# First pair in a list of its own ahead of the loop, second pair's turns placed earlier in PE's list, and the small tables made on GpSimd

## The chip, the cores and the metric

The kernel runs on one core of one Trainium2 chip. The metric is the device time of one execution in microseconds (us). Before the change it is 121.83 us, the median of 8 runs (121.37 to 122.72).

Engines are called by short names here: PE (TensorE, matrix multiplies), DVE (VectorE), ACT (ScalarE), POOL (GpSimd) and SP (SyncE, which issues DMAs here and nothing else). Each works through its own list of instructions in order, and waits where an instruction needs what another engine or a DMA has not delivered.

## What is computed

A linear attention with decay (RWKV5) feeds a soft mixture of experts. Cut to what matters:

```python
# r, k, v: (4, 8, 768, 48) float32;  w, u: (8, 48)
for t in range(S):
    cur = einsum('bhd,bhe->bhde', u * k[:, :, t], v[:, :, t])
    y[:, :, t] = einsum('bhd,bhde->bhe', r[:, :, t], state + cur)
    state = w[..., None] * state + einsum('bhd,bhe->bhde', k[:, :, t], v[:, :, t])

x = y.transpose(0, 2, 1, 3).reshape(3072, 384)
logits = x @ phi                                  # 3072 x 32 slots
d = softmax(logits, axis=0)                       # dispatch
slot_in = (d.T @ x).reshape(8, 4, 384)
slot_out[e] = relu(slot_in[e] @ w1[e]) @ w2[e]    # w1: 8 x 384 x 1024, w2: 8 x 1024 x 384
out = softmax(logits, axis=1) @ slot_out          # 3072 x 384
```

Each softmax adds 1e-9 to its sum. The inputs are k, r, v (14.2 MB), w1 and w2 (25.2 MB) and some small ones; the output is 4.7 MB.

## The kernel before

The recurrence is not run step by step. For two heads at a time (a *pair*, 96 channels) k and r are scaled by powers of the decay, so that the state's decay becomes a product of two tables, and chunks of 128 positions are handled by matrix multiplies. A batch has four pairs (q = 0 to 3), four batches make 16 pairs, m = 0 to 15. A pair has 768 positions in two *halves* of three chunks; the halves are numbered i = 0 to 31.

The steps of a pair or half, by the names of their helpers:

- `tt(j, q)` and `ex(j, q)` make the decay tables, once for each q and for k (j = 0) and r (j = 1): a product on DVE (L193) and an exponential on ACT (L197), into `W`. They need `lnw`, the logarithm of w spread over all partitions by `spread` (L182 on PE, L183 on ACT).
- `scale(m, j)` (L233) multiplies k or r by its table into `kr`, on DVE for the first pair and on POOL for all others.
- `t_pe`, `t_evac`: the *turns*. PE transposes `kr` into T0 or T1 (L240), and ACT copies it into `kT` or `rT` (L246). `b_pe`, `b_evac` turn kT back (L252 on PE, L257 on DVE) into `kn`. `prod_f` (L262, DVE) multiplies the turned k and r.
- `v_cast` casts v to bf16 (L273 on POOL for the first pair, L275 on ACT for the others); `v_pe`, `v_evac` bring it into order (L289 on PE, L295 on ACT) as `vn`.
- `a_pe`, `mask_f`: products of kT and rT within a chunk (L304, PE), masked on DVE (L309) into `AT`.
- `m_pe`, `z_evac`: states (L319, L330) and the u term (L334) in `Mb`; DVE multiplies them by the table `zt` (L346) and makes the diagonal part `dv` (L347). `zt[:, q, 2]` is the table's decayed part: ACT copies `zt[:, q, 0]` scaled by `wT` (L552). `wT` and `ucol` come from w and u through one small transpose (L208) and a few tiny operations (`wu_steps`, L206).
- `y_pe`, `y_evac`: the output of a half (L357, L368, L370, then ACT L377).

The kernel writes the order of every engine's list out by hand: `O(...)` keeps instructions in the order in which the program records them. The main loop (L499) runs from i = -5 to 31. In turn i it handles a_pe and m_pe of half i + 1, y_pe of half i, v_pe of half i + 2, scale and turns of the pairs two or three ahead, and from the second batch on a piece of routing (`route`: logits, exponentials, dispatch sums) for the batch before. The negative turns are the ramp: each helper is called only if its index exists. Three small tables say what else a turn records: `T_AT` the decay tables, `Z_AT` the decayed parts of zt, and `W_AT` how many expert weights POOL issues.

Loads: SP issues all of k, r and v. A batch lies in one of three `raw` buffers; the fourth batch goes into the first one's buffer and is issued at turn 3. The sixteen expert weights (768 KB each in bf16; the DMA casts from f32) are issued by POOL, w1 into `w_all` (L140), w2 into the second and third raw buffer (L143). Ahead of the first, at turn 12, POOL copies one element of the last batch's k into `guard` (L576), so that it waits for that load. The last weight is cut into three pieces, issued behind the loop (L581).

Behind the loop come the two expert products (L628, L665), where PE takes the experts in the order of their loads, the scaling of the slots (L676), and the output in eight pieces (L689 to L709).

`keep_warm(n)` (L146) issues n matmuls of zeros whose result is not used.

Of the kernel before, what the change touches and what calls it, by code (L numbers as in the profile page):

```python
# [9 lines left out]
def kernel(  # L10
# [41 lines left out]
    def O(ins):  # L52
        return tc.keep_in_program_order(ins)
# [57 lines left out]
    O(dve.memset(warm, 0.0))  # L111
    O(dve.memset(one_f, 1.0))
    zt = cst.tile([128, nQ, 3, P2], f32, name="zt")
    O(dve.memset(zt[:], 0.0))

    def load_kr(which, src, b, h0, h1):
        O(sp.dma_start(out=raw_of(which, b).rearrange("p (h x) -> p h x", h=H)[:, h0:h1, :],
# [28 lines left out]
    def keep_warm(n, bank=Yb, data=None):  # L146
        data = warm if data is None else data
        for _ in range(n):
            O(pe.matmul(bank[:, 0:512], data[:, 0:128], data[:, 0:512], start=True, stop=True))
# [25 lines left out]
        O(dve.memset(t[:].rearrange("p a j (e s) -> p (a j e) s", s=64)[:, :, D:64], 0.0))  # L175
    ident = cst.tile([128, 128], bf, name="ident")
    O(dve.tensor_copy(ident[:], ident_f))

    keep_warm(4)

    def spread(bank, a, z):
        O(pe.matmul(bank[:, 0:z - a], one_f, w_row[:, a:z], start=True, stop=True))  # L182
        O(act.activation(out=lnw[:, a:z], in_=bank[:, 0:z - a], func=AF.Ln))  # L183
# [7 lines left out]
    def tt(j, q):  # L191
        e = (sk, sr)[j]
        O(dve.tensor_mul(W[j][:, q], lnw[:, None, q * P2:(q + 1) * P2].to_broadcast([128, J, P2]),  # L193
                         e[:, :, None].to_broadcast([128, J, P2])))

    def ex(j, q):
        O(act.activation(out=W[j][:, q], in_=W[j][:, q], func=AF.Exp))  # L197

    tt(0, 0)
    tt(1, 0)  # L200
    spread(Vb, P2, H * D)
    ex(0, 0)
    ex(1, 0)
    wT = cst.tile([128, nQ], f32, name="wT")

    def wu_steps(n):  # L206
        if n == 0:
            O(pe.transpose(Mb[:, 0:8], wu[:], ident_f[0:8, 0:8]))  # L208
            O(act.activation(out=wT[:], in_=Mb[:, 0:4], func=AF.Ln))
            O(act.activation(out=wT[:], in_=wT[:], func=AF.Exp, scale=float(T)))  # L210
            O(dve.tensor_copy(wuT[:], Mb[:, 0:8]))
        if n == 1:
            O(dve.tensor_mul(ucol[0:64, :, 0], wuT[0:64, 0:4], wuT[0:64, 4:8]))
            O(dve.tensor_mul(ucol[64:128, :, 1], wuT[64:128, 0:4], wuT[64:128, 4:8]))

    O(pool.memset(zt[0:64, :, :, 0:D], 1.0))
    O(pool.memset(zt[64:128, :, :, D:P2], 1.0))
    ones = cst.tile([128, 128], bf, name="ones")
    Le_t = [cst.tile([128, L, 128], bf, name=f"Le{j}") for j in range(2)]
    phi_s = cst.tile([128, nM, ES], bf, name="phi_s")  # L220
# [7 lines left out]
    def scale(m, j):  # L228
        b, q = divmod(m, nQ)
        kr = kr_t[m % NKR]  # L230
        src = raw_of(j, b).rearrange("p (h j d) -> p j h d", h=H, j=J)[:, :, 2 * q:2 * q + 2, :]
        eng = dve if m == 0 else pool
        O(eng.tensor_mul(kr[:, j].rearrange("p j (h s) -> p j h s", s=64)[:, :, :, 0:D], src,  # L233
                          W[j][:, q].rearrange("p j (h d) -> p j h d", h=2)))

    def t_pe(m, j):
        kr = kr_t[m % NKR]
        bank = (T0, T1)[j]
        for x in range(J):
            O(pe.transpose(bank[:, x * C:(x + 1) * C], kr[:, j, x, :], ident[:]))  # L240
# [8 lines left out]
    def b_pe(m):  # L249
        kT = st["kT", m]  # L250
        for c in range(nC):
            O(pe.transpose(T0[:, c * C:(c + 1) * C], kT[:, c * C:(c + 1) * C], ident[:]))  # L252

    def b_evac(m):
        kn = wk.tile([128, nC, C], bf, name="kn", bufs=2)
        st["kn", m] = kn
        O(dve.tensor_copy(kn[:].rearrange("p c t -> p (c t)"), T0[:, 0:S]))  # L257
# [34 lines left out]
    def v_evac(i):  # L292
        vn = wk.tile([128, L, 2, D], bf, name="vn", bufs=3)
        st["v", i] = vn
        O(act.copy(vn[:].rearrange("p c e d -> p (c e d)"), Vb[:, 0:L * P2]))  # L295
# [146 lines left out]
    def route(i, part):  # L442
# [23 lines left out]
        if s < 2 * L:  # L466
            xt_ev(*ch[s])

    pend = []
    W_AT = {12: 1, 13: 1, 14: 1, 15: 1, 17: 1, 19: 1, 20: 1, 22: 1, 23: 1, 25: 1, 26: 5}  # L470
    T_AT = {-4: [(tt, 0, 1), (tt, 1, 1), (ex, 0, 1), (tt, 0, 2)], -3: [(ex, 1, 1), (ex, 0, 2)],
            -1: [(tt, 1, 2), (ex, 1, 2)], 0: [(tt, 0, 3), (ex, 0, 3)], 1: [(tt, 1, 3), (ex, 1, 3)]}
    Z_AT = {-3: 0, -1: 1, 1: 2, 2: 3}
    nw = 0
    n0, n1 = nG - 2, nG - 1
    Wf = [t[:].rearrange("p q j d -> p (q j d)") for t in W]
# [18 lines left out]
                O(pe.matmul(lg[:, c, :], xs[:, n - n0, mi, c, :], phi_s[:, mi, :],  # L495
                            start=(mi == 0 and c == 0), stop=(mi == nM - 1), skip_group_check=True))

    keep_warm(5)
    for i in range(-5, nH):  # L499
        mu, odd = divmod(i, 2)  # L500
        if 0 <= i + 1 < nH:
            a_pe(i + 1)
            mask_f(i + 1)
        if pend:
            disp_ev(*pend.pop())
        if i == nH - 1:
# [1 line left out]
            disp(n0 - 1, ds_t)  # L508
            le_t(n0 - 1)
            let_ev(n0 - 1, None, dve)  # L510
        if 0 <= i < nH:
            y_pe(i)
            y_evac(i)
        if 0 <= i + 2 < nH:
            v_pe(i + 2)
            v_evac(i + 2)
        if 0 <= i + 1 < nH:
            m_pe(i + 1)
            z_evac(i + 1)
        if odd == 0 and 0 <= mu + 1 < nU:  # L520
# [9 lines left out]
        if 0 <= mu + 2 < nU:  # L530
            t_pe(mu + 2, odd)
            route(i, 1)
            t_evac(mu + 2, odd)
            if odd and i < 0:
                b_pe(mu + 2)
                b_evac(mu + 2)
        else:
            route(i, 1)
        if odd == 0 and 0 <= mu + 2 < nU:
# [5 lines left out]
            turn(n1, (0, 1), T1, act)  # L545
        for f, j, q in T_AT.get(i, ()):
            f(j, q)
        if i in (-4, -3):
            wu_steps(i + 4)
        if i in Z_AT:  # L550
            q = Z_AT[i]
            O(act.activation(out=zt[:, q, 2, :], in_=zt[:, q, 0, :], func=AF.Copy, scale=wT[:, q:q + 1]))  # L552
        if i == 2:
            O(pool.memset(ones[:], 1.0))
            for t in Le_t:
# [184 lines left out]
```

The softmax here doesn't subtract the row's maximum and nothing guards it: scores larger than these inputs give would overflow.

## Time and profile before

| what | value |
|---|---|
| median of 8 runs | 121.83 us |
| the profiled execution's own time | 121.37 us |
| its span in the trace | 119.6 us |
| busy in the span: PE, DVE, ACT, POOL | 101.4, 94.9, 83.6, 59.2 us |
| DMA written: by SP's queue (q1), by POOL's (q0) | 16.03 MB, 15.34 MB |
| read from HBM, written to HBM | 39.38 MB, 4.72 MB |
| first half's output (L357) starts | 14.15 us |
| first weight load issued by POOL | 37.99 us |
| first expert product (L628) starts | 91.22 us |
| last matmul of the second expert product | 103.02 us |

The span begins with the first instruction and ends with the last; 1.77 us of the execution's own time lie around it. Busy times of different engines overlap, so they say how full an engine is and not what sets the end. What sets the end is read from three views: the *chain of waits*, which starts at the last instruction and follows back, step by step, what released it; the *windows*, which give each engine's busy time, the granted PE clock, the busy share of the 16 DMA engines and the GB/s that they wrote in a stretch of the span; and the *timeline*, which lists instructions in order with the idle time ahead of each and what ended it. Where an instruction waited for several things, the idle time is put down to one of them.

### The profile page before, as it was taken

The numbers are of one execution on the slowest core, as the hardware profiler recorded it, in microseconds if no ns is written. First come the engines' busy times: TensorE is split into PE (matmuls) and PEld (weight loads), VectorE is DVE, ScalarE is ACT, GpSimd is POOL, SyncE is SP. The second block draws the span as 40 slices with busy tenths as digits, with TensorE's granted clock in tenths as the row PEclk, the third lists the DMA queues.
The fourth block names the chain that finished last, engine by engine and source line by source line (L and its number), as shares of the span: only waits on it lengthen the run. The fifth ranks groups of instructions, "written<-read, shape, count | busy, mean of one in ns | idle before, by whom it ended". The sixth has DMA issues, their size and how long they took to land.

```text
span 119.6 us, 4336 instructions
## 1 busy us (share of the span) xinstructions
PE 101.4 (85%) x1797; PEld 81.7 (68%) x1797; DVE 94.9 (79%) x187; ACT 83.6 (70%) x183; POOL 59.2 (50%) x70
## 2 busy tenths in 40 slices
PE   5897877799999999999999999999979996795000
PEld 1455766578988888898888888888865686682000
DVE  6889999999999999899999899999943510499000
ACT  4259887998979988888898988988954500398000
POOL 7426744699999999796877592111000000011100
PEclk9999999999999999999999999999999999999755
DMA  3999999999999999999999999999999998179991
GB/s 98 341 345 367 377 374 371 348 389 362 319 387 381 343 218 223 211 219 210 221 212 219 214 214 216 216 213 214 215 216 213 220 205 146 18 288 386 428 407 70
DMA packets 20797, 31.79 MB, mean 266 GB/s; under 512 B 1129, under 2 KB 17898, under 8 KB 20650
## 3 DMA queue, kind: packets, MB, share of 16 engines
q0 software_dynamic: 2960, 15.34, 57.1%
q1 hardware_dynamic: 17648, 16.03, 39.7%
q8 instruction: 14, 0.23, 0.7%
q10 hardware_dynamic: 170, 0.15, 0.4%
q14 instruction: 5, 0.04, 0.1%
HBM read 39.38 MB, written 4.72 MB: 369 GB/s over the span
## 4 chain that ended last, share of the span: by engine, by line
PE 39%; DMA 21%; DVE 19%; ACT 7%; issue 6%; DVEq 0%; POOLq 0%; ACTq 0%
DMA raw<-in_moe_w_dram 21%; PE Vb L289 6%; PE T L240 5%; PE Ab L304 4%; PE Yb L357 4%; DVE W L193 3%; DVE prod L262 3%; PE Mb L330 3%; PE T L252 3%; DVE AT L309 2%; DVE raw L691 2%; PE Yb L370 2%; ACT rT L246 2%; DVE dv L347 2%; PE Xb L392 2%
## 5 line engine op out<-in xcount | busy, mean ns | idle before, releaser
L233 POOL TENSOR_TENSOR kr<-raw,W 128x576 bf16<-128x576 f32 x30 | 41.9, 1413 | 13.7 <-ACT W L197 5.0
L309 DVE TENSOR_TENSOR AT<-Ab,mask_ut 128x768 bf16<-128x768 f32 x32 | 30.3, 947 | 0.8 <-PE Ab L304 0.6
L289 PE MATMUL Vb<-v_bf,Q 128*128 128x96 bf16 x288 | 17.5, 206 | 0.4 <-ACT vn L295 0.4
L240 PE MATMUL T<-ident,kr 128*128 128x128 bf16 x192 | 16.6, 225 | 0.9 <-POOL kr L233 0.9
L289 PEld LDWEIGHTS <-Q 128*128 128x128 bf16 x288 | 15.8, 98 | 1.8 <-issue 0.4
L246 ACT COPY kT<-T 128x768 bf16<-128x768 bf16 x16 | 12.8, 801 | 4.5 <-PE T L240 3.3
L246 ACT COPY rT<-T 128x768 bf16<-128x768 bf16 x16 | 12.8, 803 | 3.4 <-PE T L240 2.8
L262 DVE TENSOR_TENSOR prod<-T,kT 128x768 bf16<-128x768 bf16 x16 | 15.2, 949 | 0.0
L347 DVE TENSOR_TENSOR dv<-vn,Mb 128x288 bf16<-128x288 bf16 x32 | 14.1, 442 | 0.0
L295 ACT CAST vn<-Vb 128x288 bf16<-128x288 f32 x32 | 13.4, 419 | 0.1
L240 PEld LDWEIGHTS <-kr 128*128 128x128 bf16 x192 | 12.2, 100 | 1.7 <-POOL kr L233 1.0
L346 DVE TENSOR_TENSOR Z<-Mb,zt 128x288 bf16<-128x288 f32 (+1 forms) x32 | 12.7, 398 | 0.8
L377 ACT CAST x<-Yb 128x288 bf16<-128x288 f32 x32 | 13.1, 409 | 0.2 <-PE Yb L370 0.2
L709 POOL DMA_DIRECT2D out_dram<-W x1 | 0.6, 552 | 24.9 <-DVE W L691 24.9
L304 PE MATMUL Ab<-rT,kT 64*128 64x128 bf16 x192 | 10.9, 219 | 2.0 <-DVE AT L309 2.0
L330 PE MATMUL Mb<-vn,kn 128*128 128x96 bf16 (+2 forms) x80 | 11.2, 238 | 0.0
L357 PE MATMUL Yb<-vn,AT 128*128 128x48 bf16 x192 | 10.3, 185 | 0.1
L275 ACT CAST v_bf<-raw 128x576 bf16<-128x576 f32 x15 | 10.2, 678 | 0.0
L143 POOL DMA_DIRECT2D raw<-in_moe_w_dram x10 | 5.5, 558 | 7.8 <-DMA raw<-in_moe_w_dram 2.9
L357 PEld LDWEIGHTS <-AT 128*128 128x128 bf16 x192 | 7.1, 96 | 3.3
L304 PEld LDWEIGHTS <-kT 64*128 64x128 bf16 x192 | 5.5, 94 | 5.5 <-DVE AT L309 1.9
L370 PE MATMUL Yb<-dv,ident 128*128 128x288 bf16 x32 | 9.1, 284 | 0.2
(143 smaller groups left out, 220.3 us busy)
## 6 DMA issues: line engine op xcount, KB each, us to landing
w_all<-in_moe_w_dram POOLq DMA_DIRECT2D x8, 768.0 KB, 13.7
raw<-in_moe_w_dram POOLq DMA_DIRECT2D x7, 768.0 KB, 18.8
raw<-in_v_dram SPq DMA_DIRECT2D x12, 288.0 KB, 7.3
raw<-in_r_dram SPq DMA_DIRECT2D x8, 288.0 KB, 5.0
raw<-in_k_dram SPq DMA_DIRECT2D x2, 1152.0 KB, 9.9
raw<-in_r_dram SPq DMA_DIRECT2D x2, 1152.0 KB, 9.4
raw<-in_k_dram SPq DMA_DIRECT2D x7, 288.0 KB, 5.7
out_dram<-raw POOLq DMA_DIRECT2D x1, 1536.0 KB, 6.7
```

The source lines that it names most:

```text
L233: O(eng.tensor_mul(kr[:, j].rearrange("p j (h s) -> p j h s", s=64)[:, :, :, 0:D], src, W[j][:, q].rearrange("p j (h d) -> p j h d", h=2)))
L240: O(pe.transpose(bank[:, x * C:(x + 1) * C], kr[:, j, x, :], ident[:]))
L246: O(act.copy(t[:].rearrange("p (s j) -> p s j", j=J), bank[:, 0:S].rearrange("p (j s) -> p s j", j=J)))
L262: O(dve.tensor_mul(pr[:].rearrange("p (s j) -> p s j", j=J), T1[:, 0:S].rearrange("p (j s) -> p s j", j=J), st["kT", m][:].rearrange("p (s ...
L289: O(pe.matmul(Vb[:, c * P2:(c + 1) * P2], Q3[:, o:o + C], vb[:, :, g, j, :], start=(j == 0), stop=(j == JV - 1)))
L295: O(act.copy(vn[:].rearrange("p c e d -> p (c e d)"), Vb[:, 0:L * P2]))
L304: O(pe.matmul(Ab[:, e, c * C:(c + 1) * C], kT[s, t], rT[s, t]))
L309: O(dve.tensor_mul(AT[:], Ab[:, :, 0:T].rearrange("p e (c t) -> p e c t", c=L), mask_ut[:, None, None, :].to_broadcast([128, 2, L, C])))
L330: O(pe.matmul(o, kn[:, g * L + c, :], vc, start=first, stop=True, skip_group_check=True))
L347: O(dve.tensor_mul(dv[:], st["v", i][:].rearrange("p c e d -> p (c e) d"), Mb[:, 288:288 + 2 * L, None].to_broadcast([128, L * 2, D])))
L357: O(pe.matmul(Yb[:, o:o + D], AT[:, e, c, :], vn[:, c, e, :], start=first, stop=False, skip_group_check=True))
L377: O(act.copy(st["x", n][:, :, q * P2:(q + 1) * P2], Yb[:, 0:L * P2].rearrange("p (c e) -> p c e", c=L)))
```

## The change

The ramp is taken out of the loop. The loop now starts at i = 0, and what the negative turns did (with some of turn 0) is written out ahead of it as one list. In that list:

- `prod_f(0)` stands ahead of `b_evac(0)` and the first `mask_f` directly behind them; a_pe and mask_f of half 1, y_pe of half 0, m_pe of half 1 and the turns and `b_pe` of pair 1 have places of their own. `t_pe(1, 0)` is recorded ahead of `a_pe(1)`, `t_pe(1, 1)` behind `y_pe(0)`.
- The tables of q = 2 (`tt(0, 2)`, `tt(1, 2)`) are recorded behind the second mask_f and the second z_evac.
- The small transpose stands between the turns of k and r. Its result is copied once to `wuT` by DVE; `wT` is made from wuT, and the two products into `ucol` are POOL's, no longer DVE's.
- The decayed part of zt for q = 0 is made in the list, and for q = 1, 2, 3 at the ends of turns 0, 1, 2 (before at turns -3, -1, 1, 2).

Ahead of the list, DVE no longer clears all of zt early; it clears the two thirds that need it behind the copy of the identity, and POOL's two memsets of ones cover the same two thirds and stand behind the first v_cast. `ex(0, 0)` is recorded ahead of the second `spread`. The zero matmuls are two and three, before four and five. In `W_AT` the issues from turn 17 on stand one turn later. DMAs on SP's and ACT's queues are as before, in the same order.

```diff
--- before.py
+++ after.py
@@ -111,7 +111,6 @@
     O(dve.memset(warm, 0.0))
     O(dve.memset(one_f, 1.0))
     zt = cst.tile([128, nQ, 3, P2], f32, name="zt")
-    O(dve.memset(zt[:], 0.0))
 
     def load_kr(which, src, b, h0, h1):
         O(sp.dma_start(out=raw_of(which, b).rearrange("p (h x) -> p h x", h=H)[:, h0:h1, :],
@@ -175,8 +174,9 @@
         O(dve.memset(t[:].rearrange("p a j (e s) -> p (a j e) s", s=64)[:, :, D:64], 0.0))
     ident = cst.tile([128, 128], bf, name="ident")
     O(dve.tensor_copy(ident[:], ident_f))
-
-    keep_warm(4)
+    O(dve.memset(zt[:, :, 0:2, :], 0.0))
+
+    keep_warm(2)
 
     def spread(bank, a, z):
         O(pe.matmul(bank[:, 0:z - a], one_f, w_row[:, a:z], start=True, stop=True))
@@ -198,23 +198,15 @@
 
     tt(0, 0)
     tt(1, 0)
+    ex(0, 0)
     spread(Vb, P2, H * D)
-    ex(0, 0)
     ex(1, 0)
+    keep_warm(3)
     wT = cst.tile([128, nQ], f32, name="wT")
 
-    def wu_steps(n):
-        if n == 0:
-            O(pe.transpose(Mb[:, 0:8], wu[:], ident_f[0:8, 0:8]))
-            O(act.activation(out=wT[:], in_=Mb[:, 0:4], func=AF.Ln))
-            O(act.activation(out=wT[:], in_=wT[:], func=AF.Exp, scale=float(T)))
-            O(dve.tensor_copy(wuT[:], Mb[:, 0:8]))
-        if n == 1:
-            O(dve.tensor_mul(ucol[0:64, :, 0], wuT[0:64, 0:4], wuT[0:64, 4:8]))
-            O(dve.tensor_mul(ucol[64:128, :, 1], wuT[64:128, 0:4], wuT[64:128, 4:8]))
-
-    O(pool.memset(zt[0:64, :, :, 0:D], 1.0))
-    O(pool.memset(zt[64:128, :, :, D:P2], 1.0))
+    def decay(q):
+        O(act.activation(out=zt[:, q, 2, :], in_=zt[:, q, 0, :], func=AF.Copy, scale=wT[:, q:q + 1]))
+
     ones = cst.tile([128, 128], bf, name="ones")
     Le_t = [cst.tile([128, L, 128], bf, name=f"Le{j}") for j in range(2)]
     phi_s = cst.tile([128, nM, ES], bf, name="phi_s")
@@ -467,10 +459,9 @@
             xt_ev(*ch[s])
 
     pend = []
-    W_AT = {12: 1, 13: 1, 14: 1, 15: 1, 17: 1, 19: 1, 20: 1, 22: 1, 23: 1, 25: 1, 26: 5}
-    T_AT = {-4: [(tt, 0, 1), (tt, 1, 1), (ex, 0, 1), (tt, 0, 2)], -3: [(ex, 1, 1), (ex, 0, 2)],
-            -1: [(tt, 1, 2), (ex, 1, 2)], 0: [(tt, 0, 3), (ex, 0, 3)], 1: [(tt, 1, 3), (ex, 1, 3)]}
-    Z_AT = {-3: 0, -1: 1, 1: 2, 2: 3}
+    W_AT = {12: 1, 13: 1, 14: 1, 15: 1, 18: 1, 20: 1, 21: 1, 23: 1, 24: 1, 26: 1, 27: 5}
+    T_AT = {0: [(tt, 0, 3), (ex, 0, 3)], 1: [(tt, 1, 3), (ex, 1, 3)]}
+    Z_AT = {0: 1, 1: 2, 2: 3}
     nw = 0
     n0, n1 = nG - 2, nG - 1
     Wf = [t[:].rearrange("p q j d -> p (q j d)") for t in W]
@@ -495,10 +486,62 @@
                 O(pe.matmul(lg[:, c, :], xs[:, n - n0, mi, c, :], phi_s[:, mi, :],
                             start=(mi == 0 and c == 0), stop=(mi == nM - 1), skip_group_check=True))
 
-    keep_warm(5)
-    for i in range(-5, nH):
+
+    scale(0, 0)
+    scale(0, 1)
+    v_cast(0)
+    O(pool.memset(zt[0:64, :, 0:2, 0:D], 1.0))
+    O(pool.memset(zt[64:128, :, 0:2, D:P2], 1.0))
+    tt(0, 1)
+    tt(1, 1)
+    t_pe(0, 0)
+    t_evac(0, 0)
+    O(pe.transpose(Mb[:, 0:8], wu[:], ident_f[0:8, 0:8]))
+    t_pe(0, 1)
+    t_evac(0, 1)
+    O(dve.tensor_copy(wuT[:], Mb[:, 0:8]))
+    ex(0, 1)
+    b_pe(0)
+    a_pe(0)
+    v_pe(0)
+    prod_f(0)
+    b_evac(0)
+    mask_f(0)
+    O(pool.tensor_mul(ucol[0:64, :, 0], wuT[0:64, 0:4], wuT[0:64, 4:8]))
+    O(pool.tensor_mul(ucol[64:128, :, 1], wuT[64:128, 0:4], wuT[64:128, 4:8]))
+    scale(1, 0)
+    ex(1, 1)
+    scale(1, 1)
+    v_evac(0)
+    O(act.activation(out=wT[:], in_=wuT[:, 0:4], func=AF.Ln))
+    O(act.activation(out=wT[:], in_=wT[:], func=AF.Exp, scale=float(T)))
+    decay(0)
+    m_pe(0)
+    z_evac(0)
+    t_pe(1, 0)
+    t_evac(1, 0)
+    a_pe(1)
+    mask_f(1)
+    v_pe(1)
+    v_evac(1)
+    y_pe(0)
+    y_evac(0)
+    tt(0, 2)
+    t_pe(1, 1)
+    t_evac(1, 1)
+    ex(0, 2)
+    v_cast(1)
+    m_pe(1)
+    z_evac(1)
+    b_pe(1)
+    tt(1, 2)
+    ex(1, 2)
+    b_evac(1)
+    scale(2, 0)
+
+    for i in range(nH):
         mu, odd = divmod(i, 2)
-        if 0 <= i + 1 < nH:
+        if 0 < i < nH - 1:
             a_pe(i + 1)
             mask_f(i + 1)
         if pend:
@@ -508,13 +551,13 @@
             disp(n0 - 1, ds_t)
             le_t(n0 - 1)
             let_ev(n0 - 1, None, dve)
-        if 0 <= i < nH:
+        if i > 0:
             y_pe(i)
             y_evac(i)
         if 0 <= i + 2 < nH:
             v_pe(i + 2)
             v_evac(i + 2)
-        if 0 <= i + 1 < nH:
+        if 0 < i < nH - 1:
             m_pe(i + 1)
             z_evac(i + 1)
         if odd == 0 and 0 <= mu + 1 < nU:
@@ -531,9 +574,6 @@
             t_pe(mu + 2, odd)
             route(i, 1)
             t_evac(mu + 2, odd)
-            if odd and i < 0:
-                b_pe(mu + 2)
-                b_evac(mu + 2)
         else:
             route(i, 1)
         if odd == 0 and 0 <= mu + 2 < nU:
@@ -545,11 +585,8 @@
             turn(n1, (0, 1), T1, act)
         for f, j, q in T_AT.get(i, ()):
             f(j, q)
-        if i in (-4, -3):
-            wu_steps(i + 4)
         if i in Z_AT:
-            q = Z_AT[i]
-            O(act.activation(out=zt[:, q, 2, :], in_=zt[:, q, 0, :], func=AF.Copy, scale=wT[:, q:q + 1]))
+            decay(Z_AT[i])
         if i == 2:
             O(pool.memset(ones[:], 1.0))
             for t in Le_t:
```

## The prediction

> **What bounds the kernel now.** I read the chain of waits first, then the windows, because a share of busy time says nothing about which wait ends last. The chain's pieces from 77 us on:
>
> ```profile
> 77.55 24.86 DMA raw<-in_moe_w_dram
> ...
> 102.44 0.24 PE Xb L665
> ...
> 103.22 0.43 DVE W L676
> ```
>
> Columns are start, length, what. From 77.55 to 102.4 the chain is one weight load; PE's last expert (L665) starts when it lands, and 17.2 us of scaling and output stand behind it. Is that load late because it was issued late, or because the DMA engines are full? The windows answer (stretch and length; busy us of PE, PEld, DVE, ACT, POOL with their instructions; granted clock; DMA share; GB/s written):
>
> ```profile
> 12.00:15.00 3.00, 2.60 (x55) 2.37 (x54) 2.86 (x6) 2.63 (x6) 2.09 (x2) 1.00 1.11 378
> ...
> 24.00:27.00 3.00, 2.91 (x59) 2.29 (x57) 3.00 (x8) 2.80 (x7) 3.00 (x4) 1.00 1.09 389
> ...
> 45.00:48.00 3.00, 2.93 (x58) 2.35 (x54) 2.94 (x6) 2.73 (x6) 3.00 (x3) 1.00 1.02 212
> ...
> 75.00:78.00 3.00, 2.99 (x61) 2.57 (x58) 3.00 (x7) 2.76 (x7) 0.47 (x2) 1.00 1.03 211
> ...
> 96.00:99.00 3.00, 2.63 (x82) 2.26 (x74) 0.14 (x2) 0.00 (x0) 0.00 (x0) 1.00 1.04 208
> 99.00:102.00 3.00, 2.30 (x24) 1.92 (x24) 0.00 (x0) 0.00 (x0) 0.00 (x0) 1.00 0.72 128
> ```
>
> The share is above 1 in every 3 us from 3 to 99 us (between 1.01 and 1.17). Up to some 42 us the engines bring k, r and v, then the weights at a flat 211 to 225 GB/s written, which is twice that read, as the weights are cast from f32 to bf16 on the way. The bytes agree: 14.2 MB of k, r, v and 12.6 MB of weights written by 102 us. It is one gapless stream, and its sum sets 102.4. Third, the timelines of PE and of POOL near it (start, length, what, and in brackets the idle time before it and its releaser):
>
> ```profile
> 98.24 0.39 PE L149 MATMUL Ab<-w_all 128*128 128x512 bf16 x1
> 99.18 0.24 PE L665 MATMUL Xb<-raw,W 128*32 128x192 bf16 x1 [0.56 <-DMA raw<-in_moe_w_dram]
> ...
> 101.05 0.24 PE L665 MATMUL Xb<-raw,W 128*32 128x192 bf16 x1 [0.39 <-DMA raw<-in_moe_w_dram]
> ...
> 102.44 0.24 PE L665 MATMUL Xb<-raw,W 128*32 128x192 bf16 x1 [0.57 <-DMA raw<-in_moe_w_dram]
> ```
>
> ```profile
> 74.48 0.54 POOL L143 DMA_DIRECT2D raw<-in_moe_w_dram  x1 [2.36 <-ACT kT L246]
> 77.55 0.53 POOL L143 DMA_DIRECT2D raw<-in_moe_w_dram  x1 [2.53 <-ACT xT L401]
> 80.96 0.53 POOL L143 DMA_DIRECT2D raw<-in_moe_w_dram  x1 [2.88 <-DMA raw<-in_moe_w_dram]
> ```
>
> PE is through with its covered work at 98.62 and then waits three times. Its remaining 32 matmuls, at the 0.083 us between starts from 99.18 on, need 2.65 us; undisturbed they would end at 101.27, and the last one starts at 103.02 and ends with the chain at 103.2. PE thus has about 1.9 us to spare. POOL's last three issues wait too; ACT, named twice, is not what they need: in POOL's list every weight load from the ninth on waits for the one eight before it to land, and a load is 3.66 us of stream (768 KB, or 0.786 MB, at 215 GB/s). So the last loads are paced by the stream itself.
>
> **The change part by part.** All of it lies ahead of the main loop or at POOL's issues, so I ask two things: how much earlier or later the loop runs, and whether the stream notices.
>
> DVE, front. The zt memset (1.02 us at 1.58) goes, and a memset of two thirds of it comes behind the ident copy: 0.68 us. DVE idled 0.48 us before its first L193 at 4.67, waiting for ACT's Ln at 4.38, which waits for the w row's DMA (issued at 1.18). Cost 0; without that cover, 0.68. The Ln does not move unless PE's L182 at 3.64 really waited for DVE, as the page's releaser says (a gain up to 1.02); its list names the DMA and the memset that ended at 1.40, so I take 0.
>
> ACT, front. ex(0,0) goes ahead of the second Ln and can start when L193 ends at 5.43 instead of 5.81: L233's first product moves from 6.41 to about 6.15, the second not (ex(1,0) ends at 7.1 as before). So DVE is again free at 7.9.
>
> DVE to mask(0). Before, L309 starts at 12.28. After: two L193 at 0.74, wuT 0.15, prod 0.96, kn 0.56 from 7.9 make 10.9. The third L193 stands behind mask(1) now, and ucol's two products (0.73 and 0.16) are POOL's. mask(0) is 1.3 us earlier, and nothing ahead of it is late: rT no longer waits behind ex(0,1), so a_pe(0) is done by about 10.4.
>
> POOL. The zt memsets (0.60 and 0.57, now two thirds: 0.8 together) go behind v_cast, which ends at 6.62; POOL idled from there to 9.75. Cost 0. The ucol products on POOL have no row: two between 0.18 each (the guard copy of one element, L576) and 1.41 each (L233, 576 elements). With 4 elements a partition I take the low end, 0.4, at about 9.5; the first scale waits for ex(0,1) until about 10.3, so they are hidden, and at the high end (2.8) scale(1,0) is 2 us late, which POOL's idle 2.02 us before 16.11 takes back.
>
> ACT behind it. Up to ex(0,3) the list has the same rows as before in another order: from 7.95, eleven evacuations and casts (five at 0.8, four at 0.4, two at 0.69), five exps at 0.68, wT and zt 0.74. They sum to 11.1 us, less some 0.05 of overlap at each of eighteen joins: ex(0,3) ends between 18.2 (nothing waits) and 20.0 (with the 0.71, 0.22 and 0.85 that ACT waited before its exps at 15.35, 18.37 and 21.19), against 19.05. It releases scale(3,0) at 19.13, and ex(1,3) behind it the scale at 21.95, after which POOL's list runs back to back to the guard at 37.86. So the guard and the first weight load (37.99) move by between -0.9 and +0.9; I take -0.4, nearer the gapless end, as mask(0) and Z(0) run ahead. PE's loop gets the same -0.4, between -1.3 (mask(0)'s gain kept whole) and, as pair 2's tables are made later, the bad end of the third rival below.
>
> Warm-up matmuls, nine to five, each 0.46 us: PE's L240 waits for DVE (0.59 us before 7.29), not for them, so their time is worth 0. The clock is the risk: six transposes take 0.82 to 0.85 us up to 9.96 and 0.49 to 0.51 from 11.23. If the step came 3.3 us later, the some 55 matmuls from 11.23 to 14.52 would cost up to 0.32 per six more: 2.9 us, less the 1.3 us that PE idles from 9 to 15 us: at most 1.6 late. The Trainium skill, "TensorE: Matmul & The Clock Gate", "What's actually happening", says that the array runs at half clock until it was busy for a window of about 3.4 us, which speaks against removing early matmuls; by it the sum would be 1.6 at PE and still 0 at the end, as 1.9 is spare.
>
> W_AT. From i=17 on the issues move one turn later (about 2.1 us). The stream wrote 11.96 MB from 45 to 102 us, so 0.7 of a load was in at 45; at 58.59, where the eighth is issued, 0.7 and 13.6 / 3.66 make 4.4 in. Seven issued less 4.4 is the smallest backlog: 2.6 loads, 9.3 us; a turn less leaves 7.2. Cost 0. Nothing queued behind them on POOL suffers: the last scale precedes the five at i=27, and the memset of uns (0.79 us at 71.33) is read at 90.95. SP's list is unchanged.
>
> What does the stream gain from weights issued 0.4 earlier? Only an overlap with the last v loads. From 38 to 42 us it wrote 362, 359, 335 and 321 GB/s: 1.38 MB. If 1.18 MB are v at the 300 GB/s seen at 31 to 33 us (297 and 308) and 0.20 weights at 214, that is 4.87 us of separate work done in 4: 0.87 over about 2.5 us of overlap, 0.35 per us. So -0.14, with 0 and -0.7 (a whole turn of 2.1 earlier) as ends. The skill's "DMA: Bandwidth & Descriptors", "Issuing engines are not separate DMA queues", says that all queues' transfers interleave on the same 16 engines, so that a second queue saves only issuing time; by it this term is 0.
>
> Sum: 102.4 - 0.14 + 17.2 = 119.46 of span, and 1.77 around it (121.37 less 119.6): 121.2 for this execution, the fastest of eight. The median is 0.46 above: 121.7.
>
> **The rivals.** First, a shorter stream: the weights' start comes a whole turn earlier, and overlap pays 0.35 per us: 121.83 - 0.7 = 121.1. For it speaks the share of 1.28 from 41 to 42 us; against it, POOL's ten scales at 1.37 stand between front and guard, so that the front must gain all 2.1 us. Second, PE and not the stream holds the end, and the front's best gain arrives whole: 121.83 - 1.3 = 120.5. For it: PE is over 97% busy from 24 to 87 us; against it, three DMA waits at the end. Third, slower: pair 2's tables come late. L193 for them moves from 9.17 to behind mask(1), and its exp behind rT(1); following the rows, mask(1) ends near 13.95, L193 at 14.6, the exp at 15.5, so scale(2,0) starts at 15.5 instead of 12.65, and the turns of pair 2 at 17.0 instead of 15.19: 1.8 late. They push v_cast(2), ex(0,3) and the decay for Z(2) on ACT, which puts Z(2) at some 20.1 for 19.13: 1.0 more. If both parts stay, PE is 2.8 late, and as it has no idle to win back from 24 to 87 us, all but the spare 1.9 reaches the end: 121.83 + 0.9 = 122.7. Below 1.9 it decides nothing. Against it: the turns' evacuation kT(2) is only 0.7 late (17.5 for 16.77), and DVE has 0.9 less to do.
>
> **How the numbers follow.** No measurable change 0.62, within 0.5% (0.61 us), which is about what a measurement of this kernel can tell from none; own range 121.2 to 122.4. Shorter stream 0.14 and PE-held 0.08, together 0.22 faster; slower 0.16, of which pair 2's tables 0.10 and uneven DMA engines at the stream's end (written rate 191, 124, 70 GB/s from 99 to 102) the rest. The range 120.8 to 122.6 leaves out part of both sides.
>
> **What would show it.** Right: last weight landing at 102 to 102.7, DMA share above 1 without a gap, mask(0) near 11, the guard at 37 to 38, and PE's waits before its last experts grown by about what the loop runs earlier. Wrong: a landing below 101.7, or PE arriving after 100.5 with no DMA wait left, or a window between 45 and 99 with a share below 1 over 3 us.

## The result, and the profile after

The changed kernel takes 122.80 us, the median of 11 runs (122.49 to 123.08); the kernel before, run beside it, 121.75 us (32 runs). The ratio is 1.0087, with a 95% interval from 1.0068 to 1.0105: a loss of 0.9%, 0.2 us outside the predicted range. The profiled execution took 122.85 us with a span of 121.0, against 121.37 and 119.6. So the two profiled runs lie 1.48 us apart and the medians 1.05: the profiled run of the kernel before is the fastest of its first eight.

The chain of waits of the changed kernel (start, length, what), from the last weight on:

```profile
78.21 25.64 DMA raw<-in_moe_w_dram
103.89 0.24 PE Xb L702
104.67 0.43 DVE W L713
```

It has the same pieces as before. The last expert's matmul (L702, before L665) starts when the last weight lands, at 103.89 instead of 102.44, and the tail is as long as it was. All of the 1.45 us between these two runs lies ahead of that landing. So the question is where the one stream of loads lost it. The windows of the changed kernel (columns as in the prediction):

```profile
12.00:15.00 3.00, 3.00 (x39) 2.52 (x38) 2.43 (x5) 1.65 (x4) 1.21 (x1) 1.00 1.10 375
...
39.00:42.00 3.00, 3.00 (x62) 2.54 (x60) 3.00 (x6) 2.76 (x8) 2.97 (x5) 1.00 1.03 293
42.00:45.00 3.00, 2.98 (x61) 2.55 (x58) 3.00 (x7) 2.76 (x7) 2.98 (x4) 1.00 0.96 182
45.00:48.00 3.00, 2.97 (x67) 2.50 (x64) 3.00 (x6) 2.23 (x6) 2.96 (x4) 1.00 1.04 211
```

and two windows of the kernel before:

```profile
39.00:42.00 3.00, 2.98 (x63) 2.55 (x60) 3.00 (x6) 2.76 (x7) 2.98 (x3) 1.00 1.17 338
42.00:45.00 3.00, 2.97 (x67) 2.65 (x68) 3.00 (x8) 2.39 (x7) 2.96 (x5) 1.00 1.07 226
```

The last two columns are the DMA share and the GB/s written. From 45 us on the two kernels move the same. In the six microseconds before, the changed one wrote 45 and 44 GB/s less: 3 us times 89 GB/s is 0.267 MB, and at the weights' 215 GB/s that is 1.24 us. Up to 39 us both had written the same (13.4 MB). In steps of 1 us the changed kernel's share is below 1 from 41 to 44 us (0.90, 0.94, 0.86). The hole is where the last v loads end and the weights begin. POOL's timeline of the changed kernel shows why the weights are not there yet:

```profile
21.20 1.41 POOL L225 TENSOR_TENSOR kr<-raw,W 128x576 bf16<-128x576 f32 x1 [1.41 <-ACT W L197]
24.50 1.42 POOL L225 TENSOR_TENSOR kr<-raw,W 128x576 bf16<-128x576 f32 x1 [1.89 <-ACT W L197]
...
40.39 0.22 POOL L613 COPY guard<-raw 128x1 f32<-128x1 f32 x1
40.51 0.75 POOL L139 DMA_DIRECT2D w_all<-in_moe_w_dram  x1
```

The two scales (before at 19.13 and 21.95) are 2.07 and 2.55 late. From the second one on POOL's list is unbroken, so the guard and the first weight load are late by as much: 40.51 instead of 37.99. Both scales wait for an exponential (L197). The front of the changed kernel, timeline of all engines:

```profile
15.51 0.80 ACT L238 COPY rT<-T 128x768 bf16<-128x768 bf16 x1 [0.21 <-PE T L232]
...
16.20 0.69 ACT L197 ACTIVATE W<-W 128x576 f32<-128x576 f32 x1
16.41 0.75 DVE L193 TENSOR_TENSOR W<-LexpT,sr 128x576 f32<-128x576 f32 x1
...
16.79 0.66 ACT L267 CAST v_bf<-raw 128x576 bf16<-128x576 f32 x1
16.97 2.82 POOL L225 TENSOR_TENSOR kr<-raw,W 128x576 bf16<-128x576 f32 x2 [3.76 <-DMA raw<-in_k_dram]
...
17.50 0.54 PE L281 MATMUL Vb<-v_bf,Q 128*128 128x96 bf16 x9 [1.41 <-ACT v_bf L267]
...
18.41 2.00 DVE L193 TENSOR_TENSOR W<-LexpT,sk 128x576 f32<-128x576 f32 x1
...
18.48 0.63 PE L232 MATMUL T<-ident,kr 128*128 128x128 bf16 x6 [0.44 <-DVE prod L254]
...
19.15 0.80 ACT L238 COPY kT<-T 128x768 bf16<-128x768 bf16 x1 [0.67 <-PE T L232]
...
19.85 0.68 ACT L267 CAST v_bf<-raw 128x576 bf16<-128x576 f32 x1
...
20.33 0.95 DVE L301 TENSOR_TENSOR AT<-Ab,mask_ut 128x768 bf16<-128x768 f32 x1
20.44 0.68 ACT L197 ACTIVATE W<-W 128x576 f32<-128x576 f32 x1
```

First, `ex(0, 2)` at 16.20 stands behind the copy into rT, and the first scale of pair 2 can only follow at 16.97 (before 12.68). POOL had rested 3.76 us; the k load named as releaser is not the cause, since the scale starts 0.08 us after the exponential ends. The turn of pair 2's k (18.48, right behind that scale) and its copy (19.15) are late with it, and `ex(0, 3)` (20.44), for which the scale at 21.20 waits, stands behind that copy and a v_cast in ACT's list. Second, `v_cast(1)` (L267) stands behind the exponential at 16.20 too, and PE idles 1.41 us for it. Third, the product for q = 3 (18.41) takes 2.00 us instead of 0.75, and the mask of half 2 behind it starts at 20.33 instead of 18.26. Up to there the front was ahead: the first mask starts at 11.09 for 12.28, the second at 13.43 for 15.23.

PE's timeline at the end of the changed kernel:

```profile
100.86 0.39 PE L148 MATMUL Ab<-w_all 128*128 128x512 bf16 x1
...
103.89 0.24 PE L702 MATMUL Xb<-raw,W 128*32 128x192 bf16 x1 [0.88 <-DMA raw<-in_moe_w_dram]
```

PE has its covered work behind it 2.62 us later than before (98.24), and of three DMA waits one is left.

So there were two suspects for the end, the stream that starts late and PE, late by more than its spare 1.9 us (the prediction's third rival), and three for the lateness of the front: the tables of q = 2 and v_cast, the fewer warm-up matmuls, and the long product.

### The profile page after: what moved, and what is told of

It reads as the page before. It is cut to its first block, busy times and chain, and to the rows that moved or that the text cites. A ratio compares the mean times of both kernels' runs of the same rounds, so it can differ in the third digit from the quotient of the medians.

```text
span 121.0 us, 4323 instructions
## 1 busy us (share of the span) xinstructions
PE 102.9 (85%) x1793; PEld 83.5 (69%) x1793; DVE 95.3 (79%) x185; ACT 84.5 (70%) x183; POOL 59.4 (49%) x72
## 3 DMA queue, kind: packets, MB, share of 16 engines
q1 hardware_dynamic: 17648, 16.03, 39.3%
## 4 chain that ended last, share of the span: by engine, by line
PE 43%; DMA 23%; DVE 15%; ACT 8%; issue 3%; POOLq 0%; DVEq 0%; ACTq 0%
DMA raw<-in_moe_w_dram 21%; PE T L232 7%; PE Vb L281 7%; PE Ab L296 5%; PE Yb L349 4%; PE Mb L322 3%; DVE prod L254 3%; DVE AT L301 3%; PE T L244 2%; PE Yb L362 2%; DVE raw L728 2%; ACT rT L238 2%; DMA LexpT<-in_w_dram 2%; DVE W L193 2%; PE Yb L360 2%
## 5 line engine op out<-in xcount | busy, mean ns | idle before, releaser
L281 PE MATMUL Vb<-v_bf,Q 128*128 128x96 bf16 x288 | 18.5, 213 | 1.4 <-ACT v_bf L267 1.4
L281 PEld LDWEIGHTS <-Q 128*128 128x128 bf16 x288 | 16.5, 102 | 3.2 <-issue 1.7
L232 PE MATMUL T<-ident,kr 128*128 128x128 bf16 x192 | 17.3, 231 | 0.8 <-DVE prod L254 0.4
L232 PEld LDWEIGHTS <-kr 128*128 128x128 bf16 x192 | 12.8, 103 | 2.0 <-DVE kr L225 1.4
L287 ACT CAST vn<-Vb 128x288 bf16<-128x288 f32 x32 | 13.4, 419 | 0.9 <-PE Vb L281 0.7
L322 PE MATMUL Mb<-vn,kn 128*128 128x96 bf16 (+2 forms) x80 | 11.7, 246 | 0.5 <-ACT vn L287 0.5
L296 PE MATMUL Ab<-rT,kT 64*128 64x128 bf16 x192 | 11.4, 227 | 0.6 <-DVE AT L301 0.3
L267 ACT CAST v_bf<-raw 128x576 bf16<-128x576 f32 x15 | 10.1, 676 | 0.0
L393 ACT COPY xT<-Xb 128x384 bf16<-128x384 bf16 x18 | 8.7, 484 | 0.2 <-PE Xb L384 0.2
L249 DVE COPY kn<-T 128x768 bf16<-128x768 bf16 x16 | 8.8, 550 | 0.0
```

What stands on the lines that cost most here:

```text
L281: O(pe.matmul(Vb[:, c * P2:(c + 1) * P2], Q3[:, o:o + C], vb[:, :, g, j, :], start=(j == 0), stop=(j == JV - 1)))
L296: O(pe.matmul(Ab[:, e, c * C:(c + 1) * C], kT[s, t], rT[s, t]))
L322: O(pe.matmul(o, kn[:, g * L + c, :], vc, start=first, stop=True, skip_group_check=True))
```

## The experiments

All were timed in five rounds beside the kernel before, with 12 executions each (e7 11, e8 6, e1 only 4). "First load" is when POOL issues the first weight, "last piece" when the first matmul on the last piece starts, both from one profiled run; the ratio is to the kernel before, run on the same chip, with its 95% interval.

| run | first load | last piece | median us | ratio to before |
|---|---|---|---|---|
| before | 37.99 | 102.44 | 121.5 to 121.8 | 1 |
| changed | 40.51 | 103.89 | 122.80 | 1.0087 (1.0068 to 1.0105) |
| e1: before, weights late | 42.27 | no wait shown | 124.43 | 1.0216 (1.0179 to 1.0252) |
| e2: changed, weights early | 37.48 | PE comes later | 122.15 | 1.0034 (1.0011 to 1.0056) |
| e3: changed, nine warm-ups | 39.43 | 102.64 | 121.69 | 1.0005 (0.9973 to 1.0036) |
| e4: changed, k table of q = 2 early | 39.86 | 103.10 | 122.04 | 1.0019 (0.9997 to 1.0041) |
| e5: before, five warm-ups | 39.17 | 102.65 | 121.78 | 1.0011 (0.9984 to 1.0038) |
| e6: before, weights early | 36.91 | 102.71 | 121.78 | 1.0028 (1.0006 to 1.0049) |
| e7: e3 + e4 + v_cast(1) early | 39.86 | 103.01 | 122.30 | 1.0055 (1.0032 to 1.0078) |
| e8: changed, old W_AT | 40.42 | 103.71 | 122.59 | 1.0084 (1.0054 to 1.0113) |
| e9: changed, product for q = 3 early | 41.34 | 104.55 | 122.87 | 1.0097 (1.0065 to 1.0129) |
| e10: changed, both tables and v_cast early | 38.85 | 102.50 | 121.49 | 0.9978 (0.9956 to 1.0001) |
| e11: e10 + nine warm-ups | 38.70 | 102.89 | 121.47 | 0.9998 (0.9971 to 1.0025) |
| e12: before, first load a turn later | 40.62 | 103.96 | 122.65 | 1.0061 (1.0028 to 1.0093) |

**Does a late start of the weights cost anything?** e1 delays the first five loads in the kernel before, e2 issues the first four two turns earlier in the changed one.

```diff
 (e1, before)
-    W_AT = {12: 1, 13: 1, 14: 1, 15: 1, 17: 1, 19: 1, 20: 1, ...
+    W_AT = {14: 1, 15: 1, 16: 1, 17: 1, 18: 1, 19: 1, 20: 1, ...
 (e2, changed)
-    W_AT = {12: 1, 13: 1, 14: 1, 15: 1, 18: 1, ...
+    W_AT = {10: 1, 11: 1, 12: 1, 13: 1, 18: 1, ...
```

> The kernel before, nothing of its front changed; only POOL's first weight load moves from turn 12 to turn 14 (turns 14 to 18 for the first five), so that it starts near 40.7 us, as late as in the changed kernel (40.51). If a late start of the weights alone costs the stream: a dip of the written rate between 41 and 44 us, the last weight landing near 103.8, 122.6 to 123.0 us, while PE is ready for its last experts at 98.6 as before. If the stream's sum sets the end whatever its start (the prediction's view): 121.6 to 122.0 us. If the changed kernel is late through PE alone: also 121.6 to 122.0.

> The changed kernel with its first four weight loads at turns 10 to 13, so that the first starts near 37.8 us although the loop is 2.6 us late. If stream start and PE are both in it: the stream is mended (landing near 102.4), and PE, ready at 101.2 and needing 32 matmuls of 0.083 us, holds the end at 103.8: 122.0 to 122.3 us. If the stream's start is all: 121.6 to 121.9. If it is nothing: 122.7 to 122.9.

e1 is 2.2% slower, more than expected, as its first load came at 42.27 and not at 40.7: in its profiled run POOL's long list of scales, which starts at 24.19 in the kernel before, started at 25.73, though nothing ahead of it had been changed. Its windows:

```profile
39.00:42.00 3.00, 3.00 (x67) 2.56 (x64) 3.00 (x8) 2.52 (x7) 3.00 (x3) 1.00 0.92 279
42.00:45.00 3.00, 2.98 (x64) 2.52 (x61) 3.00 (x6) 2.75 (x7) 2.96 (x5) 1.00 0.42 61
...
102.00:105.00 3.00, 2.54 (x22) 2.44 (x22) 0.00 (x0) 0.00 (x0) 0.00 (x0) 0.65 0.71 127
```

A share of 0.42 at 42 to 45 us is the same hole, deeper. In the last line PE's clock has fallen to 0.65 after a wait of 2.62 us, so part of e1's loss is that and not the stream. e2 removes the hole, and 0.65 us of the changed kernel's loss goes (122.80 to 122.15), not all: its last 32 matmuls start at 100.79 and run to 103.05 with no DMA wait among them. So both suspects are real, in an order: the late stream holds the end of the changed kernel, and PE, late too, is next, 0.3% above the kernel before. (The profiled run of e2, 121.70 us, is the fastest of its twelve.)

**From which start on?** e6 moves the first four loads of the kernel before two turns earlier, e12 its first load one turn later.

```diff
-    W_AT = {12: 1, 13: 1, 14: 1, 15: 1, 17: 1, ...
+    W_AT = {10: 1, 11: 1, 12: 1, 13: 1, 17: 1, ...   (e6)
+    W_AT = {13: 2, 14: 1, 15: 1, 17: 1, ...          (e12)
```

> The kernel before with the first four weight loads at turns 10 to 13, so that the first starts near 35.2 instead of 37.99. The prediction's first rival (a longer overlap of the two queues shortens the stream by 0.35 us per us): 0.9 less, 120.7 to 121.1 us. If the engines are full either way: 121.5 to 121.9, the last landing at 102.2 to 102.6.

> Kernel before, one edit: the guard and the first weight load move from turn 12 to turn 13, where two loads are issued; everything else is untouched, so front, PE and tables are as before. Theory (the weights have to start by about 39.4 us, and from there a later start reaches the end one for one): first load near 40.1, last piece at 102.9 to 103.4, time 122.2 to 122.7. Rival (a start this late costs nothing, what makes the changed kernel late is PE's work in the loop): last piece within 0.2 of 102.44, time 121.5 to 121.9.

e6 gains nothing (1.0028; its first load came at 36.91, not at the 35.2 expected): an earlier start is no shorter stream. e12, which changes nothing in the front or on PE's list, loses 0.6%, and its windows and its last piece (103.96) look like those of the changed kernel:

```profile
39.00:42.00 3.00, 3.00 (x65) 2.53 (x63) 3.00 (x7) 2.52 (x6) 2.99 (x6) 1.00 0.95 285
42.00:45.00 3.00, 2.98 (x61) 2.55 (x59) 3.00 (x6) 2.76 (x8) 2.98 (x3) 1.00 0.95 168
```

Read down the table, the last piece stays between 102.44 and 102.89 for first loads from 36.91 to 39.43; from there to 41.34 it moves from 102.64 to 104.55, 1.91 us for 1.91 us. So the kernel before, in its profiled run, had about 1.4 us to spare at the start of its weights (39.43 less 37.99), and the changed kernel's start, 2.5 later, lies 1.1 past the bend, as much as the medians differ (1.05).

That spare is not there in every run. POOL's unbroken list of scales that leads to the guard starts at 24.19 in the kernel before, but at 25.73, 25.54 and 25.47 in e1, e6 and e12, whose fronts are the same code; PE's clock fell to 0.57, 0.50 and 0.51 in them between 12 and 18 us. The first load stands 13.80 us behind that start, so with such a front the kernel before would issue it at 39.3 to 39.5, at the bend (an estimate from these rows). The three profiled runs with the changed front as it is (changed, e2, e8) start the list at 26.43 to 26.73. e12, whose front was 1.28 later in its profiled run, issued its first load 0.5 later than expected. Its twelve times reach from 121.36 to 123.16, probably because one turn sits just past the bend, where a front that varies from run to run decides; one trace can't show that.

**What makes the front late: the clock?** e3 gives the changed kernel its nine warm-up matmuls back, e5 takes four from the kernel before.

```diff
-    keep_warm(2)
+    keep_warm(4)
 ...
-    keep_warm(3)
+    keep_warm(5)
```

> The changed kernel with the zero matmuls of before (four and five, for two and three). If the late front comes from the clock: full speed from about 10.5 us, no relapse at 18 to 22, the first weight load near 38.5, 121.7 to 122.1 us. If it comes from the order (pair 2's tables and v_cast(1) late on ACT): at most 0.8 us earlier up to rT(1), PE still idle for some 1.5 us at 16 to 18, first load 39.7 to 40.2, 122.3 to 122.7 us.

> The kernel before with the changed kernel's zero matmuls (two and three, for four and five), nothing else. If they hold the clock up: six transposes still take 0.8 us until about 14.5 instead of 10, the front is some 1 us late, the first weight load starts near 39, just inside what the stream bears (up to about 39.3 by the four runs before), PE is ready at 99.6 with 0.9 to spare: 121.7 to 122.2 us. If the clock does not depend on them: full speed from 11 as before, 121.6 to 121.9.

e3 is as fast as the kernel before, and its profiled run starts the weights 1.08 earlier than the changed kernel's. That 39.43 is neither the 38.5 that was expected if the clock is the cause nor the 39.7 to 40.2 if the order is, and the clock still fell back, to 0.58 from 18 to 21 us. e5 loses nothing that can be measured. Its first load is 1.18 later than in the profiled run of the kernel before, but its list of scales starts at 25.39, no later than in e1, e6 and e12 with all nine warm-ups, so e5 does not show what the four matmuls cost the front.

What they do to PE is seen in all fourteen traces. In the seven runs with nine, a group of six transposes first takes 0.5 to 0.6 us between 8 and 12 us; in the seven with five, the groups up to 14 us still take about 0.8. But in six of the seven with nine, all but the kernel before, the clock then falls back to about 0.5 for some 3 us (with five: in the changed kernel and e2), so that part of the gain can be lost again. For the changed kernel the four are worth its whole loss in time (122.80 to 121.69), and by single traces 0.8 to 1.1 us of the front (the list of scales starts at 25.67 for 26.43 to 26.73).

**Or the tables?** e4 moves the k table of q = 2 up, e7 adds v_cast(1) and the nine warm-ups, e10 moves both tables and v_cast and keeps five warm-ups, e11 is e10 with nine.

```diff
     tt(1, 1)
+    tt(0, 2)            (e4, e7, e10, e11)
 ...
     ex(1, 1)
+    ex(0, 2)            (e4, e7, e10, e11)
 ...
     mask_f(1)
+    tt(1, 2)            (e10, e11)
     v_pe(1)
     v_evac(1)
+    v_cast(1)           (e7, e10, e11)
+    ex(1, 2)            (e10, e11)
     y_pe(0)
 ... each of them taken out of its old place
```

> The changed kernel with pair 2's k table made where it was before: its product on DVE behind the one of pair 1's r, its exponential on ACT behind ex(1, 1). If the order is the cause: scale(2, 0) starts near 13.2 for 16.97, PE's idle at 16 to 18.5 shrinks from 2.9 to under 1 us, no relapse of the clock, first weight load at 38 to 39, 121.8 to 122.2 us. If the clock is: mask(0) 0.7 later, slow matmuls up to 15 as now, 122.6 to 122.9 us.

> The changed kernel with three things of its front put back: four and five zero matmuls, pair 2's k table made behind pair 1's, and the cast of pair 1's v ahead of y_pe(0). If these are the whole cause: no idle of PE above 1 us at 14 to 17, no half clock after 11, first weight load at 37 to 38.3, and with the stream full 121.4 to 121.8 us. If something else of the change is late: first load after 39, 122 us or more.

> Changed kernel with both tables of q = 2 made as early as their inputs allow: tt(0,2) behind tt(1,1), ex(0,2) behind ex(1,1), tt(1,2) directly behind the second mask, v_cast(1) ahead of y_pe(0), ex(1,2) behind it. Warm-up matmuls stay two and three. Theory (the late tables of q = 2 and the late v_cast start POOL's scales late, POOL's unbroken list hands that to the first weight load): scale(2,1) near 16 instead of 18.4, scale(3,1) at 22.5 or before, first weight load at 38.6 or before, last piece of the weights at 102.4 to 102.7, time 121.4 to 121.8. Rival (the cold PE alone makes the front late): scale(3,1) not before 23.5, first weight load 39.5 to 40.5, time 122.0 to 122.8.

> As the run with all tables early, and the warm-up matmuls are four and five again. Theory: first weight load at 37.0 to 38.2, but the stream's sum holds the end, so the last piece still comes at 102.3 to 102.7 and the time is 121.3 to 121.8, the same as before and no gain. Rival (the front's gain arrives at the end once nothing is late): last piece below 102.0, time 120.5 to 121.2.

e4 gains 0.65 us in the start of the weights (39.86; 38 to 39 was expected) and comes to 122.04, in the range expected if the order is the cause. e7 missed its expectation: PE's idle stretch at 16 us was gone, but the weights started no earlier than in e4, because the r table of q = 2 still stood behind the second Z, which held the second scale of pair 2 until 18.06. e10 moves that table too, and POOL's timeline becomes:

```profile
16.50 1.40 POOL L225 TENSOR_TENSOR kr<-raw,W 128x576 bf16<-128x576 f32 x1 [1.41 <-ACT W L197]
19.86 1.41 POOL L225 TENSOR_TENSOR kr<-raw,W 128x576 bf16<-128x576 f32 x1 [1.96 <-PE T L232]
22.83 1.41 POOL L225 TENSOR_TENSOR kr<-raw,W 128x576 bf16<-128x576 f32 x1 [1.56 <-ACT W L197]
...
38.72 0.19 POOL L613 COPY guard<-raw 128x1 f32<-128x1 f32 x1
38.85 0.75 POOL L139 DMA_DIRECT2D w_all<-in_moe_w_dram  x1
```

The scale that was at 24.50 is at 22.83, 0.3 later than expected, and the first load at 38.85, 0.25 later than expected, but inside the spare. The hole is closed, and PE waits for the stream three times again, as before (e10, windows and PE's timeline):

```profile
39.00:42.00 3.00, 3.00 (x68) 2.64 (x65) 3.00 (x7) 2.76 (x6) 2.95 (x4) 1.00 1.14 340
42.00:45.00 3.00, 2.94 (x59) 2.43 (x57) 3.00 (x7) 2.76 (x8) 2.98 (x4) 1.00 1.10 236
```

```profile
99.42 0.26 PE L702 MATMUL Xb<-raw,W 128*32 128x192 bf16 x1 [0.25 <-DMA raw<-in_moe_w_dram]
...
101.14 0.24 PE L702 MATMUL Xb<-raw,W 128*32 128x192 bf16 x1 [0.22 <-DMA raw<-in_moe_w_dram]
...
102.50 0.24 PE L702 MATMUL Xb<-raw,W 128*32 128x192 bf16 x1 [0.55 <-DMA raw<-in_moe_w_dram]
```

121.49 us, 1.3 below the changed kernel, undoes the whole loss by the order of five calls, with the warm-ups still at five. Whether e10 is also faster than the kernel before stays open: the interval's upper end is 1.0001. e11 was expected to start the weights at 37.0 to 38.2 and did at 38.70: with the tables early, the warm-ups bring 0.15, not the 1.1 that they bring alone, and its last piece came 0.2 later than expected. In its profiled run the clock fell to 0.52 from 12 to 15 us. So a better order is remedy enough with five warm-ups (e10), and four more warm-ups are with the changed order (e3). They are not with every order: e7 has all nine and k's table early, and still loses 0.55%; in its profiled run the clock fell to 0.58 from 12 to 15 us. How much of the lateness is the clock's and how much the order's stays open, as the two do not add up.

**Or the long product?** e9 puts the product for q = 3 ahead of the time at which POOL works on pair 2.

```diff
-    T_AT = {0: [(tt, 0, 3), (ex, 0, 3)], 1: [(tt, 1, 3), (ex, 1, 3)]}
+    T_AT = {0: [(ex, 0, 3)], 1: [(tt, 1, 3), (ex, 1, 3)]}
 ...
     tt(0, 2)
+    tt(0, 3)
```

> Changed kernel, one move: the k product of the fourth pair (tt(0,3), DVE) is recorded directly behind tt(0,2), so that it is over before POOL starts its pair of scales at 17. Theory (a DVE product and a POOL product hold each other up, and this is part of what makes the weights start late): the product takes 0.75 us instead of 2.00, mask(2) starts near 19.2 instead of 20.33, scale(3,1) at 23.0 to 23.8 instead of 24.50, the first weight load at 39.0 to 39.8 instead of 40.51, and the time is 121.8 to 122.2. Rival (the long product is only idle time that something else would take): first weight load within 0.3 of 40.5, time 122.6 to 123.0.

The theory of that run finds no support: 1.0097 is no gain on 1.0087. Timeline of e9:

```profile
14.71 1.42 DVE L193 TENSOR_TENSOR W<-LexpT,sk 128x576 f32<-128x576 f32 x2
...
17.41 3.01 POOL L225 TENSOR_TENSOR kr<-raw,W 128x576 bf16<-128x576 f32 x2 [3.79 <-ACT W L197]
...
20.41 0.96 DVE L301 TENSOR_TENSOR AT<-Ab,mask_ut 128x768 bf16<-128x768 f32 x1 [1.28 <-PE Ab L296]
```

The product for q = 3 is one of the two at 14.71, 0.7 us each, and yet the mask starts at 20.41, now behind 1.28 us of waiting for PE. The time is the rival's (122.6 to 123.0), its first load is not: 41.34 is 0.83 later than in the changed kernel. The second mask was already 0.41 later in that run (13.84 for 13.43), the pair of scales now takes 3.01 instead of 2.82, where a third product runs at 17.05, and PE was slow for longer: six transposes still took 0.85 us at 22.91 (0.53 at 22.10 in the changed kernel), and 0.49 only at 25.34. So this trace is no clean test; the changed kernel's own rows say more. The long product ends at 20.41, and the exponential that needs it, at 20.44, would hardly have started sooner without it, as the v_cast ahead of that on ACT (19.85, 0.68) ends no earlier.

**And W_AT's later issues?** e8 puts the old table of issues into the changed kernel.

```diff
-    W_AT = {12: 1, 13: 1, 14: 1, 15: 1, 18: 1, 20: 1, 21: 1, 23: 1, 24: 1, 26: 1, 27: 5}
+    W_AT = {12: 1, 13: 1, 14: 1, 15: 1, 17: 1, 19: 1, 20: 1, 22: 1, 23: 1, 25: 1, 26: 5}
```

> The changed kernel with the old turns for the weight issues from turn 17 on. If moving them a turn later costs nothing (the backlog covers it, as predicted): 122.6 to 123.0 us, the landing near 103.8 as in the changed kernel. If those issues are part of the loss: 122.0 to 122.4.

1.0084 against 1.0087: the later issues cost nothing that can be measured.

## Why the prediction was wrong

What held. The stream and 17.2 us of tail set the end. The first mask came at 11.09 (10.9 predicted; the rows that it adds make 11.05). The two ucol products on POOL took 0.20 us each, at 9.50 and 9.76 (0.4 at about 9.5 predicted). W_AT's later issues cost nothing (e8). In the kernel before, five warm-ups cost nothing (e5). PE's tail starts 1.2 late there (99.42 for 98.24), inside the 1.6 allowed; e6 with all nine starts it at 99.59. Two small readings are off, and nothing hangs on them: 2.6 loads of backlog are 9.5 us and not 9.3, and the weights' rate falls to 208 GB/s in two windows and not to 211.

What failed is the step "the guard and the first weight load (37.99) move by between -0.9 and +0.9; I take -0.4". They moved by +2.5. That range came from adding up ACT's rows as if its own work, and the waits that it had before, set the time: `ex(0, 3)` was to end between 18.2 and 20.0. It ended at 21.12, because ACT now waited in new places: its exponentials stood behind copies that waited for PE's turns (0.63, 0.21 and 0.67 us at 12.99, 15.51 and 19.15), and the turns stood behind late scales or ran at half speed. The third rival had those waits (a scale of pair 2 at 15.5 instead of 12.65, the turns at 17.0); measured were 16.97 and 18.48, later still. PE was to be 2.8 late and was 2.62. But the rival's lateness was carried on to PE only, and not to the guard, though both follow from the same scales. The warm-ups were costed the same way, against PE's spare alone; in the changed kernel giving them back takes the whole loss away (e3), as a slow PE also makes the scales late (pair 2's start at 15.61 there for 16.97).

The second half of the failure is the term for the stream. It asked what an earlier start gains (-0.14, ends 0 and -0.7) and had no price for a later one. The runs give it: nothing up to a first load at about 39.4, then one for one. The changed kernel's 40.51 is 1.1 past that; the medians differ by 1.05, the hole in the windows is 1.24 and the two profiled runs' landings differ by 1.45. The gain of 0.35 us per us for an earlier start is not there at all (e6).

The rivals. A shorter stream falls (e6: weights issued two turns earlier gain nothing), and PE holding the end on the fast side falls with it. The third rival's time, 122.7, is within 0.1 of the measured 122.80, but it is right by another road: in the changed kernel PE still waits 0.88 us for the stream. What PE's lateness alone costs shows in e2: 122.15, a lateness of 2.62 less the spare 1.9 being 0.7, or 122.5 by that rival's own sum (121.83 and 0.7).

The signs named beforehand: a guard after 38 and a landing after 102.7 did tell that it was wrong; the test for a share below 1 did not, since it looked from 45 us on and the hole lies at 41 to 44.

## What to carry to other kernels

When a stream of transfers fills the whole time, look for every instruction that *starts* a part of it, and give each a spare as one gives it to an engine: when does the part before run dry, and how late may this one be? An unbroken list between a late wait and that instruction, here ten scales of POOL, hands the lateness on whole, twenty microseconds away from its cause. And when a rival's lateness is worked out, follow it along all the engines that wait for it, not only along the one that the rival is about. A spare read from one trace is that trace's: here it is 1.4 us in the profiled run, and next to nothing with the fronts of three others.

## What the runs showed of the hardware

**The clock can fall when PE is half busy, not only when it rests.** The changed kernel, windows of its front:

```profile
15.00:18.00 3.00, 1.59 (x26) 1.36 (x24) 2.28 (x6) 2.79 (x5) 1.03 (x1) 1.00 1.12 379
18.00:21.00 3.00, 2.56 (x34) 2.04 (x33) 3.00 (x3) 2.28 (x5) 1.79 (x2) 0.62 1.08 367
21.00:24.00 3.00, 3.00 (x53) 2.67 (x51) 2.52 (x6) 2.04 (x6) 1.41 (x1) 0.81 1.10 372
```

After 3 us with PE busy for 1.59, the clock was 0.62 and then 0.81. e11 and e12 show the same from 12 to 15 us (0.52 and 0.51) after windows with 1.48 and 1.39 busy; the kernel before, with 2.40, 2.35 and 2.13 busy in the three windows from 15 to 24 us, kept 1.00. The Trainium skill, "TensorE: Matmul & The Clock Gate", "What's actually happening", names an idle window of about 3.4 us as what throttles, in a grid that runs free of the kernel. The variation from run to run agrees with a free grid; that a half-busy stretch can be enough is this case's measurement. It is no threshold: e8 kept 1.00 with 1.46 of 3 us busy (16 to 19 us), and in e1 the clock fell at about 14 us, with 2.31 and 2.15 busy in the windows from 9 to 15 us. e8, whose profiled run did not fall back, took as long as the changed kernel (122.59), so falling back alone does not make the loss.

**The record of the clock does not show the slow start.** It says 1.00 for the changed kernel from 12 to 15 us, where the six transposes at 14.65 take 0.82 us; the six of L244 at 15.60 take 0.49. In e9 it says 1.00 throughout from 9 to 27 us, where six transposes took 0.80 to 0.85 up to 22.91. The speed of a cold PE is read from the length of equal groups of matmuls.

**A product on DVE and one on POOL can hold each other up.** L193 took 2.00 us beside POOL's scale of 2.82 for two, and about 0.75 in the changed kernel's other rows; in e3 the pair of scales took 3.57 instead of 2.82, where the product ran its 0.75. The Trainium skill, "Perfetto Trace Analysis", "Optimizing Scalar/DVE Operations", says that the two engines share a read port of SBUF; the trace agrees that one waits, and does not show for what. Moving the product did not shorten the time here (e9).
